# Strided sparse attention into a PReLU feed-forward: batch 0 in another order and layout, weights cast by the DMA, warm-up matmuls

## The chip, the cores and the metric

The kernel runs on one core of a Trainium2 chip. The metric is the device time of one execution in microseconds (us). The kernel before took 391.42 us, the median of three runs from 390.7 to 391.8. A profiled execution of it gives the trace that is read here.

A core has a matrix engine (TensorE, PE in the rows; PEld is its loading of weights), a vector engine (VectorE, DVE), an activation engine (ScalarE, ACT), a general engine (GpSimd, POOL) and an engine that mostly issues transfers (SyncE, SP). Each works through its own instructions in order. Transfers run on 16 DMA engines that all queues share. SBUF is the memory in which all of them work; PSUM is where TensorE writes its results.

## The reference

For 8 batches, 8 heads, 576 positions and a head width of 64, heads 0 to 3 attend locally (a query sees itself and the 31 positions before it) and heads 4 to 7 with a stride (a query sees the positions at or before it that have the same remainder by 32). The result of shape 4608 x 512 goes through a feed-forward with a PReLU.

```python
mask_local = (rel >= 0) & (rel < stride)                       # stride = 32
mask_strided = (rel >= 0) & (pos[None, :] % stride == pos[:, None] % stride)
scores = np.where(masks[None], scale * q @ k.T, -1e9)
attn = softmax(scores) @ v                                     # 8 x 8 x 576 x 64
x = attn.transpose(0, 2, 1, 3).reshape(4608, 512)
h = x @ w_in                                                   # 512 -> 2048
g = np.maximum(h, 0.0) + alpha * np.minimum(h, 0.0)
out = g @ w_out                                                # 2048 -> 512, float32
```

All inputs are float32; the kernel computes its products on float16 operands.

## The kernel before

**Pairs and pieces.** Two heads of a batch make a pair: pairs `4b` and `4b+1` are batch b's local ones, `4b+2` and `4b+3` its strided ones. A pair goes through pieces, and each piece is a handful of instructions on several engines:

- T (`transpose_piece`, L191): TensorE transposes the float16 q or k; ACT copies k into `kT` (L198), DVE copies q into two halves of `qpad` (L202).
- Sc (`score_piece`, L204): scores in PSUM (`sp`, L212), ACT takes the exponential into `et` (L220), and POOL multiplies with a mask (L222, L226). Each pair has three.
- Pv (`pv_piece`, L229): matmuls with v and a column of ones (L240); DVE takes the reciprocal of the sums (L247) and scales (L249). A local pair has two, a strided pair three.
- X (`x_piece`, L254): TensorE transposes the result, and a copy puts it into `xT`, the transposed input of the feed-forward: ACT for a strided pair, with a step of 8 elements in the write (L261), DVE for a local one (L265).

Strided heads are loaded with 8 neighbouring positions in a partition, so that positions that share a remainder by 8 end up in one block of 72; local heads are loaded with position `96 j + p` in partition p, block j.

**Loads.** `load_part` (L102) brings q, k or v of four heads of a batch into a staging tile. Of strided heads it reads runs of 2 KB (8 positions of 64 floats) in two DMAs; of local q and k it reads runs of 256 bytes in four DMAs, one for each head; of local v runs of 256 bytes in five DMAs, with overlapping windows of 128 positions. `cast_part` (L143) casts a staging tile to float16, in two halves. Weights are loaded in four chunks of 1 MB each (`load_w`, L431) into the same ring of seven staging tiles, and cast by DVE, ACT or POOL (`cast_w`, L440).

**Feed-forward.** The 4608 tokens are cut into 9 chunks of 512. `lin1_piece` (L386) computes 128 of the 2048 hidden units for a chunk: four matmuls into one of two `hps` buffers, then ACT writes the negative part (`neg`, L406) and DVE combines both into `gT` (L409), which frees the buffer. `lin2_piece` (L415) computes a quarter of one 128-row tile of the output into `ops`, which has one buffer; after the fourth quarter ACT copies it to SBUF (`osb`, L426) and SP stores it.

**Order.** The order of every engine is that of the program. Ahead of everything come memsets and the loads of batch 0: local q and k on SP, local v on ACT's queue, then strided q, k and v and w_in on SP (L449 to L466). Batch 0's pieces run local pairs first (L287 to L311); POOL's masks and the casts of w_in lie in between. Batch 1's loads are issued on SP after piece 20 and at the end of batch 0, w_out's after them (L494), and batch 2's local ones behind these.

From batch 1 on a fixed rotation (L325 to L366) interleaves the pieces of neighbouring pairs, with POOL's casts for the next data between them; after the second half of a cast the next batch's load of that tile is issued on SP. The first lin1 (chunk 0) is interleaved with batch 1 (L507 to L513), the second with batch 2 (L515 to L519); then lin2 of chunk 0, and from L526 on lin2 of chunk n and lin1 of chunk n+1 alternate with attention. Chunk 1 needs the end of batch 0 and most of batch 1, so lin1 of chunk 1 needs batch 1's last X piece, that of pair 7. By the rotation that piece comes after the scores of pair 8 and the first scores of pair 9.

Of the kernel before, what the change touches and what calls it, by code (L numbers as in the profile page):

```python
# [9 lines left out]
F32 = mybir.dt.float32  # L10
# [20 lines left out]
def kernel(  # L31
# [17 lines left out]
    RING = 4 * S  # L49

# [39 lines left out]
    for i in range(3):  # L90
        keep(nc.vector.memset(qpads[i][64:128, 0, :], 0.0))
        keep(nc.vector.memset(qpads[i][0:64, 1, :], 0.0))
        keep(nc.vector.memset(kTs[i][:, 576:640], 0.0))
    for t in vls + vss:
        keep(nc.gpsimd.memset(t[:, :, :, 64:65], 1.0))
    for t in ets:
        keep(nc.gpsimd.memset(t[:, 384:512], 0.0))
# [4 lines left out]
    def load_part(b, strided, nm, eng=None):  # L102
# [3 lines left out]
        if strided:  # L106
            for lo, hi in ((0, 64), (64, 72)):
                keep(eng.dma_start(
                    st[lo:hi, :].rearrange("p (h e) -> p h e", h=4),
                    src[b, 4:8, 8 * lo : 8 * hi, :].rearrange("h (p t) d -> p h (t d)", t=8),  # L110
                ))
        elif nm != "v":
            for h in range(4):
                keep(eng.dma_start(  # L114
                    st[0:96, 384 * h : 384 * h + 384].rearrange("p (j d) -> p j d", j=6),
                    src[b, h, :, :].rearrange("(j p) d -> p j d", p=96),
                ))
# [25 lines left out]
    def cast_part(b, strided, nm, pr, eng):  # L143

        st = loaded[(b, strided, nm)]
        n = 8 if strided else 6
        np_ = 72 if strided else 96
# [12 lines left out]
        else:  # L160
            if (b, strided, nm) not in cast16:
# [3 lines left out]
            w = 128 * n  # L165
            cast_copy(
                eng,
                t16[0:np_, pr, 0:w].rearrange("p (t h d) -> p t h d", t=n, h=2),
                st[0:np_, w * pr : w * pr + w].rearrange("p (h t d) -> p t h d", h=2, t=n),
# [21 lines left out]
    def transpose_piece(P, which):  # L191
        src = cast16[(P.b, P.strided, which)]
        tp = pspool.tile([128, 1024], F16, tag="ps", name=f"t{which}")
        for t in range(P.n):
            keep(nc.tensor.transpose(  # L195
                tp[:, P.w * t : P.w * t + P.w], src[0 : P.w, P.pr, 128 * t : 128 * t + 128], ident[0 : P.w, 0 : P.w]))
        if which == "k":
            keep(nc.scalar.copy(P.kT[:, 0:576], tp[:, 0:576]))  # L198
        else:
            for hh in range(2):  # L200
                r0 = 64 * hh
                keep(nc.vector.tensor_copy(P.qpad[r0 : r0 + 64, hh, :], tp[r0 : r0 + 64, 0:576]))  # L202

    def score_piece(P, i):  # L204
# [15 lines left out]
        keep(nc.scalar.activation(et[0:r, 0:n], sp[0:r, 0:n], AF.Exp, scale=SCALE))  # L220
        if not P.strided and i == 0:
            keep(nc.gpsimd.tensor_tensor(et[:, 0:n], et[:, 0:n], mfirst, op=ALU.mult))  # L222
        else:
            m = mstr if P.strided else mother
            ev = et[0:r, 0:n].rearrange("r (c f) -> r c f", f=w)
            keep(nc.gpsimd.tensor_tensor(  # L226
# [27 lines left out]
    def x_piece(P):  # L254
# [5 lines left out]
        if P.strided:  # L260
            keep(nc.scalar.copy(  # L261
                xT[:, P.hp, base : base + S].rearrange("r (p t) -> r t p", t=8),
                xp[:, 0:576].rearrange("r (t p) -> r t p", t=8)))
# [23 lines left out]
    for g in (0, 1):  # L287
        feed(T(g, "q"), 0)
        feed(T(g, "k"), 0)
    for i in range(3):  # L290
        feed(Sc(0, i), 0)
    for i in range(3):
        feed(Sc(1, i), 0)
    for g in (0, 1):
        for i in range(2):
            feed(Pv(g, i), 0)
# [3 lines left out]
    feed(X(0), 0)  # L300
    feed(X(1), 0)
# [3 lines left out]
    for g in (2, 3):  # L305
        for i in range(3):
            feed(Pv(g, i), 0)
        if g == 3:
            feed(X(2), 0)
    feed(X(3), 3)  # L310
# [104 lines left out]
    def lin2_piece(n, i):  # L415
        mt, part = i // 4, i % 4
        if part == 0:
            ops_cur["t"] = popool.tile([128, 512], F32, tag="ops", name="ops")
        ops = ops_cur["t"]
        for kf in range(4 * part, 4 * part + 4):  # L420
# [3 lines left out]
        if part == 3:  # L424
            osb = opool.tile([128, 512], F32, tag="osb", name="osb")
            keep(nc.scalar.copy(osb, ops))  # L426
            r0 = 512 * n + 128 * mt
            keep(nc.sync.dma_start(out[r0 : r0 + 128, :], osb))


    def load_w(c, second):  # L431
        st = spool.tile([128, 2048], F32, tag="st", name="wst")
        if second:
            src = moe_w_out[512 * c : 512 * c + 512, :].rearrange("(kf p) c -> p kf c", p=128)
        else:
            src = moe_w_in[:, 512 * c : 512 * c + 512].rearrange("(kk p) c -> p kk c", p=128)
        keep(nc.sync.dma_start(st.rearrange("p (kk c) -> p kk c", kk=4), src))
        return st

    def cast_w(c, second, st, half, eng):  # L440
        s = st.rearrange("p (kk c) -> p kk c", kk=4)[:, 2 * half : 2 * half + 2, :]
        if second:
            o = wout16[:, 4 * c + 2 * half : 4 * c + 2 * half + 2, :]
        else:
            o = win16[:, 2 * half : 2 * half + 2, 512 * c : 512 * c + 512]
        cast_copy(eng, o, s)


    keep(nc.scalar.dma_start(ident, id_dram))  # L449
    load_part(0, False, "q")  # L450
    load_part(0, False, "k")
# [3 lines left out]
    load_part(0, False, "v", nc.scalar)  # L455
    load_part(0, True, "q")
    load_part(0, True, "k")
    load_part(0, True, "v")
    wi = [load_w(0, False)]
    cast_part(0, False, "q", 0, "dve")  # L460
    cast_part(0, False, "k", 0, "act")
    cast_part(0, False, "q", 1, "dve")
    cast_part(0, False, "k", 1, "act")
    cast_part(0, False, "v", 0, "pool")
    cast_part(0, False, "v", 1, "pool")
    wi += [load_w(1, False), load_w(2, False), load_w(3, False)]  # L466
    apt = pspool.tile([128, 512], F32, tag="ps", name="apt")
    keep(nc.tensor.transpose(apt[:, 0:16], alpha_r, id16))
    keep(nc.vector.tensor_scalar(oma, apt[:, 0:16], -1.0, 1.0, op0=ALU.mult, op1=ALU.add))

    for i in range(end0):
        if i == 14:
            cast_part(0, True, "q", 0, "dve")
            cast_part(0, True, "k", 0, "act")
            cast_part(0, True, "q", 1, "dve")
            cast_part(0, True, "k", 1, "act")
            cast_part(0, True, "v", 0, "pool")
            cast_part(0, True, "v", 1, "pool")
        attn_step(end0)
        if i == 20:  # L480
            for nm in ("q", "k", "v"):
                load_part(1, False, nm)
        if i == 24:
            cast_w(0, False, wi[0], 0, "dve")
            cast_w(0, False, wi[0], 1, "act")
    cast_w(1, False, wi[1], 0, "dve")
    cast_w(1, False, wi[1], 1, "act")
    for nm in ("q", "k", "v"):
        load_part(1, True, nm)
    cast_w(2, False, wi[2], 0, "dve")  # L490
    cast_w(2, False, wi[2], 1, "act")
    cast_w(3, False, wi[3], 0, "pool")
    cast_w(3, False, wi[3], 1, "pool")
    wo = [load_w(c, True) for c in range(4)]  # L494
# [4 lines left out]

    for nm in ("q", "k", "v"):  # L500
        for pr in range(2):
            cast_part(1, False, nm, pr, "pool")
        load_part(2, False, nm)
# [3 lines left out]
    for m in range(16):  # L507
        lin1_piece(0, m)
        attn_n(1, end1)
        if m >= 4:  # L510
            attn_n(1, end1)
# [3 lines left out]
    for m in range(16):  # L515
        if m % 2 == 0:
            cast_w(m // 4, True, wo[m // 4], (m // 2) % 2, "pool")
# [48 lines left out]
```

## Time and profile before

| what | before |
|---|---|
| median of 3 runs | 391.42 us (390.7 to 391.8) |
| the profiled execution | 391.96 us |
| its span, first to last instruction | 390.2 us |
| TensorE busy | 329.5 us (84%) |
| ACT, DVE, POOL busy | 213.8, 197.9, 175.8 us |
| moved by DMA | 48.31 MB, mean 124 GB/s |

The profile is of one execution. A row of a group names the line, the engine, the operation and the tiles written and read, then shapes and the count; after the bar come its busy time, the mean of one in ns, and how long the engine idled just before, with what ended the wait. The slices cut the span in 40 equal parts and give tenths of busy time. The chain of waits follows the work that ended last back to the start, each step with its start and length in us. A timeline row gives start and length, and in brackets the idle time before it.

### The profile page before, as it was taken

Reading aid. Unit: us, or ns where it says so; the run is one execution under the profiler, and the core shown is the slowest. Engines: PE = TensorE matmul, PEld = TensorE weight load, DVE = VectorE, ACT = ScalarE, POOL = GpSimd, SP = SyncE. Lnnn points to the kernel's source line nnn. Section 1 sums busy time; section 2 is a strip of 40 time slices with the busy share of each in tenths; the row PEclk is TensorE's granted clock in tenths of the full one; section 3 lists DMA queues with packets and bytes.
Section 4 is the critical chain, followed back from the end, with each engine's and each line's share of the span. In section 5 each row is a group of like instructions: output and inputs, shape, how many; then the busy total and the mean of one; then the engine's idle time right before and its main releaser. Section 6 shows DMA issues by size and latency. Waiting matters only on the chain.

```text
span 390.2 us, 6743 instructions
## 1 busy us (share of the span) xinstructions
PE 329.5 (84%) x2561; PEld 184.2 (47%) x2561; DVE 197.9 (51%) x401; ACT 213.8 (55%) x332; POOL 175.8 (45%) x210
## 2 busy tenths in 40 slices
PE   1464815686899899989998999899899899999985
PEld 1352412353445445555555777455455444444432
DVE  4274505383774346556556566666566444444400
ACT  2466513166565655695677557756955844444411
POOL 1654572789687546556555656665333000000000
PEclk9995778595999999999999999999999999999999
DMA  9998999988499655486558436010000001010021
GB/s 179 200 321 220 217 264 306 211 178 160 108 191 219 144 117 138 112 189 126 126 123 177 110 87 157 21 55 29 28 29 29 27 29 54 27 55 28 27 82 54
DMA packets 80384, 48.31 MB, mean 124 GB/s; under 512 B 64592, under 2 KB 64736, under 8 KB 80352
## 3 DMA queue, kind: packets, MB, share of 16 engines
q1 hardware_dynamic: 76848, 46.94, 51.4%
q10 hardware_dynamic: 3504, 0.95, 1.4%
q8 instruction: 20, 0.33, 0.4%
q14 instruction: 12, 0.10, 0.1%
HBM read 38.43 MB, written 9.44 MB: 123 GB/s over the span
## 4 chain that ended last, share of the span: by engine, by line
PE 67%; DMA 14%; ACT 6%; POOL 5%; DVE 3%; issue 2%; SPq 2%; ACTq 0%; POOLq 0%
PE ops L421 29%; PE hps L396 28%; DMA wst<-in_moe_w_in_dram 5%; DMA stv<-in_v_dram 4%; ACT xT L261 4%; DMA stq<-in_q_dram 3%; PE pv L240 3%; PE sp L212 3%; SPq L114 2%; PE xp L257 2%; DVE gT L409 2%; PE tq L195 2%; DMA stk<-in_k_dram 2%; POOL et L226 2%; PE tk L195 1%
## 5 line engine op out<-in xcount | busy, mean ns | idle before, releaser
L396 PE MATMUL hps<-xT,win 128*128 128x512 f16 (+1 forms) x640 | 156.8, 371 | 11.5 <-ACT xT L261 9.2
L421 PE MATMUL ops<-wout,gT 128*128 128x512 f16 x576 | 145.3, 379 | 4.6 <-ACT osb L426 4.6
L409 DVE SCALAR_TENSOR_TENSOR gT<-neg,oma,hps 128x512 f16<-128x512 f32 x144 | 106.9, 743 | 82.2 <-ACT neg L406 81.5
L406 ACT ACTIVATE neg<-hps 128x512 f32<-128x512 f32 x144 | 88.0, 611 | 92.5 <-PE hps L396 91.6
L226 POOL TENSOR_TENSOR et<-et,masks 128x384 f16<-128x384 f16 (+2 forms) x80 | 72.2, 910 | 77.6 <-ACT et L220 76.9
L396 PEld LDWEIGHTS <-win 128*128 128x128 f16 x640 | 59.6, 101 | 48.1 <-issue 10.3
L421 PEld LDWEIGHTS <-gT 128*128 128x128 f16 x576 | 51.9, 97 | 52.8 <-issue 6.1
L220 ACT ACTIVATE et<-sp 128x384 f16<-128x384 f32 (+2 forms) x96 | 47.7, 510 | 15.3 <-PE sp L212 14.5
L247 DVE RECIPROCAL rc<-pv 96x6 f32<-96x6 f32 (+2 forms) x80 | 15.0, 187 | 71.9 <-PE pv L240 71.8
L261 ACT COPY xT<-xp 128x576 f16<-128x576 f16 x16 | 43.6, 2754 | 13.8 <-PE xp L257 13.3
L240 PEld LDWEIGHTS <-et 72*128 72x128 f16 (+1 forms) x448 | 25.5, 102 | 44.1 <-POOL et L226 18.9
L249 DVE TENSOR_TENSOR x<-pv,rc 96x384 f16<-96x384 f32 (+2 forms) x80 | 42.1, 527 | 2.7
L202 DVE COPY qpad<-tq 64x576 f16<-64x576 f16 x64 | 29.0, 453 | 12.4 <-PE tq L195 11.9
L426 ACT COPY osb<-ops 128x512 f32<-128x512 f32 x36 | 21.0, 585 | 25.6 <-PE ops L421 24.4
L212 PE MATMUL sp<-qpad,kT 128*128 128x144 f16 (+1 forms) x224 | 32.6, 253 | 2.3 <-ACT xT L261 1.9
L212 PEld LDWEIGHTS <-kT 128*128 128x128 f16 x224 | 21.2, 105 | 22.7 <-issue 5.7
L240 PE MATMUL pv<-vl,et 128*128 128x65 f16 x192 | 13.6, 208 | 20.0 <-POOL et L226 14.3
L139 POOL CAST q<-stq 96x768 f16<-96x768 f32 (+1 forms) x28 | 25.4, 929 | 10.9 <-DMA stq<-in_q_dram 8.6
L198 ACT COPY kT<-tk 128x576 f16<-128x576 f16 x32 | 20.4, 637 | 12.4 <-PE tk L195 12.4
L139 POOL CAST k<-stk 96x768 f16<-96x768 f32 (+1 forms) x28 | 26.0, 928 | 1.3 <-DMA stk<-in_k_dram 1.2
L139 POOL CAST vl<-stv 128x768 f16<-128x768 f32 x16 | 13.1, 836 | 14.8 <-DMA stv<-in_v_dram 14.8
L222 POOL TENSOR_TENSOR et<-et,masks 128x384 f16<-128x384 f16 x16 | 14.5, 909 | 11.2 <-ACT et L220 11.2
(29 smaller groups left out, 152.2 us busy)
## 6 DMA issues: line engine op xcount, KB each, us to landing
out_dram<-osb SPq DMA_DIRECT2D x36, 256.0 KB
stq<-in_q_dram SPq DMA_DIRECT2D x32, 144.0 KB
stk<-in_k_dram SPq DMA_DIRECT2D x32, 144.0 KB
stv<-in_v_dram SPq DMA_DIRECT2D x28, 160.0 KB
stq<-in_q_dram SPq DMA_DIRECT2D x8, 512.0 KB
stk<-in_k_dram SPq DMA_DIRECT2D x8, 512.0 KB
stv<-in_v_dram SPq DMA_DIRECT2D x8, 512.0 KB
wst<-in_moe_w_in_dram SPq DMA_DIRECT2D x4, 1024.0 KB
```

Source lines behind the costliest of these rows:

```text
L139: keep(nc.gpsimd.tensor_copy(o, i))
L202: keep(nc.vector.tensor_copy(P.qpad[r0 : r0 + 64, hh, :], tp[r0 : r0 + 64, 0:576]))
L212: keep(nc.tensor.matmul(sp[:, 2 * w * x : 2 * w * x + 2 * w], P.kT[:, k0 : k0 + 128], P.qpad[:, :, w * t : w * t + w], start=(x == 0), sto ...
L220: keep(nc.scalar.activation(et[0:r, 0:n], sp[0:r, 0:n], AF.Exp, scale=SCALE))
L226: keep(nc.gpsimd.tensor_tensor(ev, ev, m.unsqueeze(1).to_broadcast([r, n // w, w]), op=ALU.mult))
L240: keep(nc.tensor.matmul(pv[:, 65 * x : 65 * x + 65], et[0:r, c : c + 128], v16[0:r, t, 2 * P.pr + hh, :], start=(x == 0), stop=(x == nb - ...
L249: keep(nc.vector.tensor_tensor(P.x16[0:w, c0 : c0 + 64 * nb].rearrange("r (c e) -> r c e", e=64), pvv[:, :, 0:64], rc[0:w, 0:nb].unsqueeze ...
L261: keep(nc.scalar.copy(xT[:, P.hp, base : base + S].rearrange("r (p t) -> r t p", t=8), xp[:, 0:576].rearrange("r (t p) -> r t p", t=8)))
L396: keep(nc.tensor.matmul(hps[:, dst : dst + w], win16[:, kk, 128 * m : 128 * m + 128], xT[:, kk, src : src + w], start=(kk == 0 and x == 0) ...
L406: keep(nc.scalar.activation(neg, hps, AF.Relu, scale=-1.0))
L409: keep(nc.vector.scalar_tensor_tensor(gTs[n][:, m, :], neg, oma[:, m : m + 1], hps, op0=ALU.mult, op1=ALU.add))
L421: keep(nc.tensor.matmul(ops, gTs[n][:, kf, 128 * mt : 128 * mt + 128], wout16[:, kf, :], start=(kf == 0), stop=(kf == 15)))
```

## The change

- **Order of batch 0.** The strided pairs (2 and 3) come first, in loads, casts and pieces; the local ones (0 and 1) follow. All six loads go to SP's queue.
- **Layout.** Local q and k are loaded as the strided ones are, in runs of 2 KB and two DMAs. The order of positions is put right when kT and qpad are copied out of PSUM, by reading with a step. The xT copy of strided pairs now reads PSUM with the step and writes in order.
- **Weights.** With `WSW = True`, `load_w` is one DMA on POOL's queue that reads float32 and writes float16 into the final tile; no engine casts weights. The four DMAs of w_in stand between the casts of v of batch 0, those of w_out between POOL's casts of batch 1's local data.
- **Gate.** A small DMA on SP reads 16 columns of w_in's second chunk; batch 1's loads stand behind it on SP.
- **Masks of batch 0** are multiplied on DVE in place of POOL. POOL's memset of `et` is wider (224 columns in place of 128).
- **Warm-up matmuls.** 12 matmuls of 128x512 on a zero tile ahead of the first cast, 4 more after each of the first four pieces, and one after each of the next twelve.
- **lin1 of chunk 0** runs its first 12 pieces with no attention between them; the casts of batch 1's local data and the loads behind them are issued after piece 10. One attention piece follows each of the last four, and the rest of batch 1 comes after that, alone.
- **The last chunk.** lin2's tiles alternate between `ops` and `hps` buffers; the last tile is computed as two halves of 256 columns, each copied by ACT and DVE (128 columns each) and stored by its own DMA.

```diff
-        if strided:
+        if strided or nm != "v":
+            h0 = 4 if strided else 0
             for lo, hi in ((0, 64), (64, 72)):
                 keep(eng.dma_start(
                     st[lo:hi, :].rearrange("p (h e) -> p h e", h=4),
...
+                    src[b, h0 : h0 + 4, 8 * lo : 8 * hi, :].rearrange(
+                        "h (p t) d -> p h (t d)", t=8),
...
+        def move(copy, o, i):
+            if P.strided:
+                keep(copy(o, i))
+            else:
+                keep(copy(o.rearrange("r (p t) -> r p t", t=8),
+                          i.rearrange("r (t p) -> r p t", t=8)))
...
+        eng = nc.vector if P.b == 0 else nc.gpsimd
...
-                xT[:, P.hp, base : base + S].rearrange("r (p t) -> r t p", t=8),
-                xp[:, 0:576].rearrange("r (t p) -> r t p", t=8)))
+                xT[:, P.hp, base : base + S].rearrange("r (p t) -> r p t", t=8),
+                xp[:, 0:576].rearrange("r (t p) -> r p t", t=8)))
...
+            if last and mt % 2 == 1:
+                ops_cur["t"] = phpool.tile([128, 512], F32, tag="hps", name="ops2")
...
+            half = phpool.tile([128, 512], F32, tag="hps", name="ops3") if part else ops
...
+            keep(nc.scalar.copy(osb[:, 0:128], half[:, 0:128]))
+            keep(nc.vector.tensor_copy(osb[:, 128:256], half[:, 128:256]))
+            keep(nc.sync.dma_start(out[r0 : r0 + 128, c0 : c0 + 256], osb[:, 0:256]))
...
     def load_w(c, second):
+        if WSW:
+            keep(nc.gpsimd.dma_start(w_dst(c, second), w_src(c, second)))
+            return
...
+    def warm(n):
+        for _ in range(n):
+            keep(nc.tensor.matmul(wps, wrm[:, 0:128], wrm, start=True, stop=True))
...
+    for nm in ("q", "k", "v"):
+        load_part(0, True, nm)
+    for nm in ("q", "k", "v"):
+        load_part(0, False, nm)
...
+    def cast_qk(b, strided):
+        cast_part(b, strided, "q", 0, "dve")
+        cast_part(b, strided, "k", 0, "act")
+        cast_part(b, strided, "q", 1, "dve")
+        cast_part(b, strided, "k", 1, "dve")
+
+    warm(12)
+    cast_qk(0, True)
+    cast_part(0, True, "v", 0, "pool")
+    cast_part(0, True, "v", 1, "pool")
+    if WSW:
+        load_w(0, False)
     cast_part(0, False, "v", 0, "pool")
+    if WSW:
+        load_w(1, False)
     cast_part(0, False, "v", 1, "pool")
+    if WSW:
+        load_w(2, False)
+        load_w(3, False)
...
+        if i == 16:
+            cast_qk(0, False)
         attn_step(end0)
+        if i < 4:
+            warm(4)
+        elif i < 16:
+            warm(1)
...
+    if WSW:
+        gate = cpool.tile([128, 16], F16)
+        keep(nc.sync.dma_start(gate, win16[:, 0, 1008:1024]))
+    for strided in (False, True):
+        for nm in ("q", "k", "v"):
+            load_part(1, strided, nm)
...
     for m in range(16):
...
         lin1_piece(0, m)
+        if m == 10:
+            for nm in ("q", "k", "v"):
+                for pr in range(2):
+                    cast_part(1, False, nm, pr, "pool")
+                load_part(2, False, nm)
+                if WSW:
+                    load_w("qkv".index(nm), True)
+            if WSW:
+                load_w(3, True)
+        attn_n(0 if m < 12 else 1, end1)
```

More of the change, by code (lines that the diff above doesn't have):

```diff
@@ L284, in X @@
         return lambda: x_piece(pairs[g])
[L287 to L296, printed above, removed]
     for g in (2, 3):
@@ L496, in attn_n @@
+    for strided in (False, True):
+        for nm in ("q", "k", "v"):
+            load_part(1, strided, nm)
+    if not WSW:
+        for c in range(4):
+            load_w(c, True)
     def attn_n(n, end):
```

168 lines of the change are left out of this document (81 added, 87 removed).

## The prediction

> **What bounds the kernel now.** I read the slices of the page first, then cut the span into stages, and then asked the chain of waits what each stage hangs on. The slices:
>
> ```profile
> span 390.2 us, 6743 instructions
> PE   1464815686899899989998999899899899999985
> POOL 1654572789687546556555656665333000000000
> DMA  9998999988499655486558436010000001010021
> ```
>
> TensorE (PE) is full from slice 13 to the end and half idle before; DMA is full in the first ten slices (98 us). The stages, by busy time (columns: stretch, length, then PE, PEld, DVE, ACT, POOL, granted clock, DMA share, GB/s):
>
> ```profile
> 0.00:10.00 10.00, 1.91 (x19) 1.56 (x19) 3.93 (x14) 2.12 (x2) 1.89 (x16) 1.00 0.97 180
> 20.00:30.00 10.00, 6.36 (x82) 5.57 (x80) 7.71 (x18) 6.58 (x11) 5.98 (x7) 1.00 1.05 331
> 38.20:95.50 57.30, 33.98 (x278) 19.42 (x278) 25.80 (x54) 25.72 (x42) 39.10 (x46) 0.74 1.04 226
> 95.50:117.00 21.50, 19.56 (x143) 10.32 (x143) 15.21 (x28) 12.37 (x24) 16.22 (x18) 0.93 0.80 145
> 117.00:137.50 20.50, 18.00 (x155) 9.88 (x153) 7.46 (x19) 11.96 (x15) 12.88 (x15) 1.00 0.84 185
> 137.50:308.00 170.50, 164.56 (x1467) 97.71 (x1467) 104.31 (x218) 113.79 (x178) 90.57 (x101) 1.00 0.39 94
> ```
>
> DMA is busy in both of the first two rows, but with 256-byte runs (0 to 10) it moves 180 GB/s, and with mostly 2 KB runs (20 to 30) 331. From 38.2 to 95.5, TensorE works 34 of 57 us; from 137.5 on it is full. So time is to be won ahead of about 137. The chain, cut to the steps that carry it:
>
> ```profile
> 1.18 3.81 DMA stq<-in_q_dram
> ...
> 17.27 20.02 DMA wst<-in_moe_w_in_dram
> ...
> 40.85 1.72 PE hps L396 x4
> 44.95 10.96 DMA stv<-in_v_dram
> ...
> 63.16 6.86 DMA stq<-in_q_dram
> ...
> 88.54 1.99 POOL vs L139 x2
> ...
> 92.74 2.73 ACT xT L261
> ...
> 138.70 0.86 PE hps L396 x4
> ```
>
> Loads carry it to about 70 us: w_in until 37.3, batch 1's strided v until 55.9, batch 2's q (queued behind w_out) until 70.0. Then POOL carries it (casts and masks). At 92.74 + 2.73 = 95.5 the first half of the sequence ends: batch 1's last xT is written, and the second chunk of lin1 can be finished. The same four matmuls take 1.72 us at 40.85 and 0.86 at 138.70; the first is the slow clock.
>
> **The change part by part.** The costs of one instruction:
>
> ```profile
> L409 DVE SCALAR_TENSOR_TENSOR gT<-neg,oma,hps 128x512 f16<-128x512 f32 x144 | 106.9, 743 | 82.2 <-ACT neg L406 81.5
> L406 ACT ACTIVATE neg<-hps 128x512 f32<-128x512 f32 x144 | 88.0, 611 | 92.5 <-PE hps L396 91.6
> L261 ACT COPY xT<-xp 128x576 f16<-128x576 f16 x16 | 43.6, 2754 | 13.8 <-PE xp L257 13.3
> L226 POOL TENSOR_TENSOR et<-et,masks 72x432 f16<-72x432 f16 x32 | 32.0, 1003 | 13.1 <-ACT et L220 12.4
> L202 DVE COPY qpad<-tq 64x576 f16<-64x576 f16 x64 | 29.0, 453 | 12.4 <-PE tq L195 11.9
> L226 POOL TENSOR_TENSOR et<-et,masks 128x384 f16<-128x384 f16 x32 | 29.0, 909 | 38.8 <-ACT et L220 38.8
> L198 ACT COPY kT<-tk 128x576 f16<-128x576 f16 x32 | 20.4, 637 | 12.4 <-PE tk L195 12.4
> L249 DVE TENSOR_TENSOR x<-pv,rc 72x384 f16<-72x384 f32 x32 | 17.7, 553 | 1.1
> L139 POOL CAST vs<-stv 72x1024 f16<-72x1024 f32 x16 | 16.4, 1048 | 4.1 <-DMA stv<-in_v_dram 4.1
> L139 POOL CAST k<-stk 72x1024 f16<-72x1024 f32 x14 | 14.5, 1035 | 1.2 <-DMA stk<-in_k_dram 1.2
> L139 POOL CAST vl<-stv 128x768 f16<-128x768 f32 x16 | 13.1, 836 | 14.8 <-DMA stv<-in_v_dram 14.8
> L139 POOL CAST wout<-wst 128x1024 f16<-128x1024 f32 x8 | 8.3, 1036 | 0.0
> L247 DVE RECIPROCAL rc<-pv 72x6 f32<-72x6 f32 x32 | 6.0, 189 | 14.7 <-PE pv L240 14.7
> L137 DVE CAST q<-stq 72x1024 f16<-72x1024 f32 x2 | 1.3, 680 | 0.0
> ```
>
> *Loads.* A load is 0.59 MB, or 1.8 us at 331 GB/s; local v keeps 256-byte runs (0.79 MB, 4.4 us at 180). The first load of before took 3.81 us for half of that, so strided q is there at about 5.1, k at 6.9, v at 8.7, local q and k at 10.5 and 12.2, v at 17 to 19 beside the first weights. w_in (4.2 MB, 12.7 us at 331) is issued by POOL behind the strided and local v casts: chunk 0 at about 11, the others at 20 to 23; chunk 1 lands at about 25, the last at about 32. The new wait, SP's little DMA that reads win16, holds all fifteen of batch 1's DMAs until chunk 1 is there. Nobody needs them sooner: by bytes (two v at 180, 12.2 MB at 331, with half of w_out in between) they are complete at about 49, and batch 2's, which share with the rest of w_out, at about 69.
>
> *Eight DMAs on POOL's queue.* No row shows a DMA that POOL issues, nor a cast in flight. The nearest for the issue is SP's pair below: 0.68 us each; I bound it by 0.5 and 2.2 (the row of four, its waits included) and take 1, so 8 us. Against it POOL loses ten weight casts of 1.04 us. For the transfer I take the rate of the 2 KB loads (it reads the same runs and writes half), with half that rate as the other end.
>
> ```profile
> 9.98 1.36 SPq L108 DMA_DIRECT2D stk<-in_k_dram  x2
> 12.97 8.85 SPq L437 DMA_DIRECT2D wst<-in_moe_w_in_dram  x4
> ```
>
> *Batch 0.* The memsets that move behind the loads, the wider one of et on POOL and the transpose of alpha lie beside the wait for the first load or for k; without that cover they cost 2 us together. The casts of w_in leave DVE, ACT and POOL, where they stood at the end of this stage. The 12 warm-up matmuls (0.43 us each by the 1.72 row) end at about 6.3, when strided q has just been cast. The other 28 cost 0.22 to 0.43 each; four behind each transpose piece push the first score from about 9 to 12, which k's casts and copies cover in part. Scores end at 15, DVE's six masks at 16. No row has a mask on DVE; two-input work there takes 553 ns for 384 elements (L249), copies of 16-bit data 453 for 576, so 0.3 to 0.62; I take 0.45. Six times L247 + L249 (0.74) end at 20.3. Local pairs: three casts to 22.3, four qpad moves, masks, four times 0.74 and two X copies on DVE: 32.
>
> *Strided reads.* Local kT and qpad, and strided xT, now read PSUM with a step and write in order. L261, the only element-wise stepped copy, takes 2754 ns where the same size in order takes 637 (L198); there the write has the step. Which side costs the 2.1 us no row tells. [...] I take 0.64 and 0.7: what L261 shows as slow is a copy with a stepped write, and the new ones have none. [...]
>
> *lin1 of chunk 0* loses its interleaving: 12 pieces stand alone. With two hps buffers a piece costs half of PE 0.86 + ACT 0.61 + DVE 0.74 + about 0.2 of hand-over, so 1.2 us: 32 + 14.4 = 46.4. Batch 1's first score is three pieces later, its mask at 51.
>
> *Batch 1, now without lin1 beside it*, is POOL's: per pair three masks (2.73 us) and three casts (2.5 to 3.1; local q and k casts are 72x1024 now, 1.04 each). Pairs 4 to 7 take 5.9, 5.8, 5.4 and 5.8, and 2.9 of pair 8's lie ahead of batch 1's last transpose: 25.8, so 76.8; four PE pieces and an xT copy of 0.64 make 79.5. DMA is close behind (batch 2's strided v is there at 69 and is wanted at 72). Against 95.5: **-16.0**.
>
> *lin1 of chunk 1, lin2 of chunk 0.* TensorE idles 21.5 - 19.6 + 20.5 - 18.0 = 4.4 us there, with POOL casting w_out. Those casts go; POOL still has the masks. I take **-1.7**, between 0 and -4.4.
>
> *xT stalls and the end*, from the waits (total, times, longest) and the timeline:
>
> ```profile
> PE hps L396 <- ACT xT L261: 9.2, 7, 2.0
> ```
>
> ```profile
> 35.67 0.58 PE L396 MATMUL hps<-xT,win 128*128 128x512 f16 x1 [1.28 <-ACT xT L261]
> 38.23 0.59 PE L396 MATMUL hps<-xT,win 128*128 128x512 f16 x1 [1.97 <-ACT xT L261]
> 95.51 0.58 PE L396 MATMUL hps<-xT,win 128*128 128x512 f16 x1 [1.53 <-ACT xT L261]
> ...
> 374.41 3.61 PE L421 MATMUL ops<-wout,gT 128*128 128x512 f16 x16 [0.67 <-ACT osb L426]
> 386.72 0.58 ACT L426 COPY osb<-ops 128x512 f32<-128x512 f32 x1 [3.75 <-PE ops L421]
> ```
>
> Of the 9.2 us, 1.28 + 1.97 + 1.53 = 4.8 lie in the first two batches; four stalls of 1.1 remain, gone with the short copy: **-4.4**. In the last chunk three waits of 0.67 to 0.72 for osb fall away, since the tiles alternate, and the last copy of 0.58 is split: **-2.4**.
>
> **Sum.** The profiled execution took 391.96 us (span 390.2 and 1.76 around it; the median is 391.42, 0.1% less). 391.96 - 16.0 - 1.7 - 4.4 - 2.4 = 367.5.
>
> **Rivals.** *Stepped PSUM reads cost what L261 costs.* Then the 4.4 stays, X(7) ends 2.1 later, four copies of batch 0 put 8.5 on ACT ahead of the exps (about 6 not covered by DVE), and local kT stalls a little in each batch (2): 382. For it: L261's 3.7 ns an element more; against: its write is stepped too. [...]
>
> *Cast in flight is slow: slower than before.* At half rate the eight MB cost 25 us more of a DMA stage that just fits; batch 2 lands some 15 later and the first term goes: 382. It decides the sign where the last w_in chunk comes later than the first term and the others can pay, at about 71 us: 4.2 MB in 59 us, 71 GB/s. At 50 GB/s it lands at 96 and lin1 stands there: 392 + 25 = 417. For it: not one packet of before went through a software queue; against: 2 KB runs at 331 GB/s leave a factor of four. [...]
>
> *The start is shorter than that.* If DVE's masks cost 0.3 and POOL casts ahead of its masks while lin1 runs, batch 0 ends at 28 and batch 1 needs 20 us: 355. For it: POOL is free from 24 to 31; against: casts wait in one queue with masks.
>
> *The early gain is given back*: TensorE is no sooner full, because batch 1 alone takes as long as with lin1 beside it: 391.
>
> **How the numbers follow.** The sum 0.52 (own range 358 to 377); stepped reads 0.15; shorter start 0.13; half-rate casts 0.06; still slower casts 0.10; given back 0.04. The range 352 to 386 holds the first nearly whole and most of the next three, about 0.8. Within 0.3% (1.2 us, what a measurement of this kernel tells from no change) 0.03, slower 0.10, faster 0.87. The predicted time is 367.
>
> **What would show it.** Strided q cast near 5.5 us; w_in complete near 32; batch 0's last X copy near 32; lin1 pieces of chunk 0 at 1.2 us; POOL full from 51 to 77; xT and local kT copies at 0.64 us; lin1 of chunk 1 starting near 79.5; no osb wait in the last chunk. It is wrong if w_in lands after 46, if the stepped copies take 2.7 us, or if POOL waits for loads between 51 and 77.

## The result and the profile after

The changed kernel takes 376.61 us (median of 4 runs, 375.11 to 378.22), the kernel before 391.13 beside it: ratio 0.963, 95% interval [0.959, 0.967]. That is 14.5 us less; the forecast was 24.4 less, at 367. The profiled execution took 378.22, the highest of the four, 1.6 above the median; its span is 376.5 against 390.2. The page's first line and four of its slices:

```profile
span 376.5 us, 6946 instructions
PE   6768874566899999999999999999999999999996
POOL 2321646899546646557655666865433000000000
DMA  7999999999997645377547736011000001001012
GB/s 154 187 182 175 180 216 223 187 200 171 197 174 172 163 119 133 107 167 178 125 112 160 158 92 154 29 41 46 29 30 30 28 28 57 28 28 57 29 57 84
```

From the twelfth slice on (9.4 us each) TensorE's digit is 9 up to the last slice; before, eights come between. DMA is still nearly full in the first twelve slices, and it moves 154 to 223 GB/s there. The windows, cut at the ends of the changed kernel's stages (columns as in the prediction):

```profile
10.00:24.50 14.50, 10.75 (x97) 6.12 (x97) 8.09 (x24) 5.76 (x10) 4.42 (x5) 0.78 1.18 186
24.50:36.00 11.50, 8.74 (x98) 6.52 (x99) 10.52 (x24) 4.83 (x10) 2.25 (x3) 0.59 1.03 167
36.00:56.50 20.50, 16.83 (x75) 6.67 (x74) 11.89 (x16) 8.89 (x15) 10.53 (x12) 0.90 1.18 202
56.50:92.27 35.77, 19.70 (x225) 15.19 (x224) 16.92 (x38) 12.58 (x25) 30.79 (x34) 0.56 1.12 196
92.27:132.60 40.33, 36.95 (x300) 19.95 (x299) 23.88 (x46) 20.45 (x38) 23.88 (x26) 0.97 0.89 178
132.60:300.00 167.40, 167.35 (x1514) 99.34 (x1514) 110.89 (x219) 98.78 (x180) 93.24 (x101) 1.00 0.39 97
```

The last row is the visible gain: TensorE idles for 0.05 us, where the row of before (137.5 to 308) left 5.94 idle. In the third and fourth rows, lin1 of chunk 0 and batch 1, little was won. The chain of waits says why:

```profile
45.93 15.41 DMA stv<-in_v_dram
...
61.35 12.19 DMA stv<-in_v_dram
...
74.10 7.58 DMA stk<-in_k_dram
...
81.83 1.04 POOL k L132
...
90.53 1.71 PE hps L394 x4
```

Loads carry it until 81.7, twelve us longer than before (70.0): batch 1's strided v, then batch 2's v and k. I mark the start of chunk 1 by ACT's first `neg` of it, since every kernel has that row; before it stands at 96.13. ACT's timeline after, with the last xT copy of batch 1 ahead of it:

```profile
90.56 0.64 ACT L261 COPY xT<-xp 128x576 f16<-128x576 f16 x1 [3.87 <-PE xp L257]
92.27 0.60 ACT L404 ACTIVATE neg<-hps 128x512 f32<-128x512 f32 x1 [1.07 <-PE hps L394]
```

Chunk 1 starts 3.9 us sooner, where 16.0 were forecast. The other 9.8 of the 13.7 us between the two spans come after it: 1.0 up to the start of chunk 1's lin2 (137.52 before, 132.63 after), 6.5 from there to the last chunk, of which 5.9 were idle time of TensorE, and 2.35 in the last chunk. The groups by form show the copies at the price taken, and the new masks below it:

```profile
L261 ACT COPY xT<-xp 128x576 f16<-128x576 f16 x16 | 10.2, 639 | 11.5 <-PE xp L257 11.1
L191 ACT COPY kT<-tk 128x576 f16<-128x576 f16 x16 | 10.2, 638 | 14.9 <-PE tk L185 14.9
L193 DVE COPY qpad<-tq 64x576 f16<-64x576 f16 x32 | 24.1, 753 | 2.1 <-PE tq L185 1.9
L226 DVE TENSOR_TENSOR et<-et,masks 128x384 f16<-128x384 f16 x4 | 1.4, 358 | 0.2
L462 POOL DMA_DIRECT2D win<-in_moe_w_in_dram x4 | 3.2, 790 | 0.0
```

### The profile page after: what moved, and what is told of

The parts are those of the page before. It is cut to its first block, busy times and chain, and to the rows that moved or that the text cites. A ratio compares the mean times of both kernels' runs of the same rounds, so it can differ in the third digit from the quotient of the medians.

```text
span 376.5 us, 6946 instructions
## 1 busy us (share of the span) xinstructions
PE 339.6 (90%) x2681; PEld 190.4 (51%) x2681; DVE 212.4 (56%) x415; ACT 181.1 (48%) x328; POOL 167.6 (45%) x196
## 4 chain that ended last, share of the span: by engine, by line
PE 75%; DMA 11%; DVE 6%; ACT 3%; POOL 2%; issue 1%; SPq 1%; ACTq 0%; POOLq 0%; DVEq 0%
PE ops L439 32%; PE hps L394 30%; DMA stv<-in_v_dram 7%; DMA stk<-in_k_dram 4%; PE sp L211 3%; PE pv L240 3%; PE xp L257 2%; DVE gT L407 2%; DVE x L249 2%; PE tk L185 2%; PE tq L185 2%; PE wps L478 1%; PE ops L430 1%; ACT neg L404 1%; ACT et L219 1%
## 5 line engine op out<-in xcount | busy, mean ns | idle before, releaser
L226 POOL TENSOR_TENSOR et<-et,masks 128x384 f16<-128x384 f16 (+2 forms) x70 | 63.2, 907 | 70.6 <-ACT et L219 69.8
L247 DVE RECIPROCAL rc<-pv 72x6 f32<-72x6 f32 (+2 forms) x80 | 14.9, 186 | 54.0 <-PE pv L240 53.9
L249 DVE TENSOR_TENSOR x<-pv,rc 72x384 f16<-72x384 f32 (+2 forms) x80 | 42.1, 527 | 2.7
L240 PEld LDWEIGHTS <-et 72*128 72x128 f16 (+1 forms) x448 | 26.4, 104 | 29.1 <-POOL et L226 14.5
L132 POOL CAST q<-stq 72x1024 f16<-72x1024 f32 x28 | 28.2, 1036 | 11.6 <-DMA stq<-in_q_dram 11.6
L132 POOL CAST k<-stk 72x1024 f16<-72x1024 f32 x28 | 28.9, 1035 | 5.5 <-PE tk L185 2.8
L193 DVE COPY qpad<-tq 64x576 f16<-64x576 f16 x32 | 24.1, 753 | 2.1 <-PE tq L185 1.9
L132 POOL CAST vs<-stv 72x1024 f16<-72x1024 f32 x16 | 16.4, 1048 | 12.3 <-DMA stv<-in_v_dram 12.3
L240 PE MATMUL pv<-vs,et 72*128 72x65 f16 x256 | 16.9, 200 | 2.6 <-POOL et L226 2.6
L185 PE MATMUL tq<-ident,q 72*128 72x72 f16 x256 | 15.1, 207 | 4.3 <-DVE q L130 4.3
L185 PEld LDWEIGHTS <-q 72*128 72x128 f16 x256 | 13.1, 105 | 10.2 <-DVE q L130 5.4
```

Of the source, the lines that this page charges most:

```text
L132: keep(nc.gpsimd.tensor_copy(o, i))
L185: keep(nc.tensor.transpose(tp[:, 72 * t : 72 * t + 72], src[0:72, P.pr, 128 * t : 128 * t + 128], ident[0:72, 0:72]))
L193: keep(copy(o.rearrange("r (p t) -> r p t", t=8), i.rearrange("r (t p) -> r p t", t=8)))
L226: keep(eng.tensor_tensor(ev, ev, m.unsqueeze(1).to_broadcast([r, n // w, w]), op=ALU.mult))
L240: keep(nc.tensor.matmul(pv[:, 65 * x : 65 * x + 65], et[0:r, c : c + 128], v16[0:r, t, 2 * P.pr + hh, :], start=(x == 0), stop=(x == nb - ...
L249: keep(nc.vector.tensor_tensor(P.x16[0:w, c0 : c0 + 64 * nb].rearrange("r (c e) -> r c e", e=64), pvv[:, :, 0:64], rc[0:w, 0:nb].unsqueeze ...
```

## The experiments

Each diff is against the changed kernel unless it says otherwise. Both loads-only kernels (the first and the fifth) leave out all computation and store zeros.

**Loads alone.** Groups of two to four loads of each form in a row; DVE closes each load with a small copy of one of its columns.

> This kernel computes nothing of the reference and stores zeros: it only loads, in eight groups, each waited for before the next, to measure the rate of each kind of load alone. Theory 'placement' (the rate of a load hangs on which partitions it fills, so that 64 of 128 partitions get about half): (1) four loads as in the changed kernel, partitions 0-63 and 64-71, 2.36 MB: 13.8 us; (2) partitions 0-31 and 32-63, 2.10 MB: 12.3 us; (3) the same rows into partitions 0-31 and 64-95: 6.5 to 7.5 us; (4) 96 partitions with runs of 1.5 KB, 2.36 MB: 9 to 10 us. Rival 'runs' (2 KB runs get 331 GB/s, and the loads were slow in the kernel because of what else moved): (1) 7.1 us, (2) 6.3, (3) 6.3, (4) about 7.5. Both: (5) 96 partitions in 256-byte runs 13 us, (6) the w_in chunks through SP 12.7 us, (7) the same through POOL with the cast 13 to 14 us, (8) two local v, 1.57 MB, 8.7 us.

The first two groups can't be read: POOL's software DMAs waited for nothing, and their four weight transfers ran beside them. In the later groups only loads of SP's queue run. Landings in DVE's timeline: three loads of the third group (the same rows in two DMAs, into partitions 0 to 31 and 64 to 95), then two successive loads of 96 partitions in 256-byte runs, then two of local v:

```profile
33.55 0.14 DVE L56 COPY fl<-st 1x1 f32<-1x1 f32 x1 [0.83 <-DMA st<-in_q_dram]
35.80 0.14 DVE L56 COPY fl<-st 1x1 f32<-1x1 f32 x1 [2.10 <-DMA st<-in_k_dram]
38.08 0.14 DVE L56 COPY fl<-st 1x1 f32<-1x1 f32 x1 [2.14 <-DMA st<-in_q_dram]
...
59.42 0.15 DVE L56 COPY fl<-st 96x1 f32<-96x1 f32 x1 [2.70 <-DMA st<-in_q_dram]
62.23 0.15 DVE L56 COPY fl<-st 96x1 f32<-96x1 f32 x1 [2.66 <-DMA st<-in_k_dram]
...
76.12 0.15 DVE L56 COPY fl<-st 128x1 f32<-128x1 f32 x1 [0.20 <-DMA st<-in_v_dram]
79.69 0.15 DVE L56 COPY fl<-st 128x1 f32<-128x1 f32 x1 [3.42 <-DMA st<-in_v_dram]
```

A local q or k as before loads it takes 2.81 us, 210 GB/s; local v 3.57 us, 220. Short runs were not as slow as the 180 GB/s of the first ten us had made me think. The third group missed its forecast: 0.52 MB land every 2.2 to 2.3 us, so four take about 9, where 'placement' said 6.5 to 7.5. With one DMA into each half of the partitions a load gets no more than some 235 GB/s.

**Local q and k back in 96 partitions**, with 6 positions each (1.5 KB runs, one DMA), all else as changed:

```diff
+        if not strided and nm != "v":
+            keep(eng.dma_start(
+                st[0:96, 0:1536].rearrange("p (h e) -> p h e", h=4),
+                src[b, 0:4, :, :].rearrange("h (p t) d -> p h (t d)", t=6)))
...
```

> The changed kernel with local q and k in 96 partitions of 6 positions (runs of 1.5 KB, one DMA) in place of 72 partitions of 8. Theory 'placement': each of these loads takes 2.6 us in place of 3.45, so batch 0 ends 1.7 us sooner and batch 1's and 2's data by 1.7 each; POOL's local casts shrink from 1.04 to 0.82 us; lin1 of chunk 1 starts 3 to 5 us sooner: 372 to 374. Rival 'runs': the loads take as long as before or a little longer, the shorter casts bring at most 1: 375 to 377.

372.26 us, ratio 0.954 [0.950, 0.957]; chunk 1 at 87.51, 4.8 us sooner. POOL's row in batch 1's stage:

```profile
57.00:87.00 30.00, 17.47 (x193) 13.68 (x191) 15.95 (x37) 11.07 (x23) 29.22 (x34) 0.57 1.09 213
```

POOL works 29.2 of the 30 us: now it is the limit there. Two of a batch's six loads in other partitions (their casts are shorter too, 0.82 us in place of 1.04, and a transpose piece has six matmuls in place of eight) bring 4.4 us more.

**w_out's loads behind lin1 of chunk 1** (after its first four pieces, not beside batch 1's loads; the issues at piece 10 go):

```diff
         lin1_piece(1, m)
+        if m < 4:
+            load_w(m, True)
```

> The changed kernel with the four loads of w_out issued behind the first four pieces of lin1 of chunk 1 in place of between the casts of batch 1. If w_out's 4.2 MB (13 us of transfer) hold up batch 1's strided and batch 2's local loads ('share'), lin1 of chunk 1 starts 7 to 10 us sooner, w_out still lands before lin2 needs it, and the time is 367 to 370. If those loads are limited by their own target partitions and w_out only uses what they leave ('placement'), it is 374 to 377; if w_out then comes too late for lin2, 377 to 385.

376.42 us, 0.966 [0.961, 0.970]. Chunk 1 starts at 87.54, 4.7 sooner, so w_out does compete with batch 1's loads. But the chain now has

```profile
92.34 21.38 DMA wout<-in_moe_w_out_dram
```

and lin2 waits for it until 113.7: all of the gain is given back.

**Weights through staging and casts on the engines**, as before:

```diff
-    WSW = True
+    WSW = False
```

> The changed kernel with the weights loaded by SP as float32 and cast by DVE, ACT and POOL, all else as it is. 'Casting in flight brings much': 16 casts of 0.7 to 1.15 us come back, the first of them ahead of lin1: 380 to 386. 'It brings nothing, the loads of q, k and v set the pace': 374 to 379, since w_out then stands behind batch 1's loads on SP.

383.39 us, 0.982 [0.979, 0.985]; chunk 1 at 97.17. By the medians casting in flight is worth 6.8 us in this kernel, together with the order of loads that comes with it: without it there is no gate, and w_out stands on SP behind batch 1's loads.

**Loads alone, each group behind the end of the one before.** In order: 64 partitions 0 to 63; 64 partitions 32 to 95; 128; the kernel's form (64 + 8); 96; weights by SP; weights with the cast by POOL.

```python
keep(nc.sync.dma_start(st[0:64, :].rearrange("p (r e) -> p r e", r=8), flat(src, 64, 8)))
...
keep(nc.sync.dma_start(st[32:96, :].rearrange("p (r e) -> p r e", r=8), flat(src, 64, 8)))
```

> Loads alone again, stores zeros, computes nothing of the reference; this time each of seven groups starts only when the one before has wholly landed, the cast transfers too. Groups 1 to 3 read the same rows of 2 KB, three times 1.05 MB: into partitions 0-63, into 32-95, into 0-127. Theory 'placement by halves' (partitions 0-63 and 64-127 are served by different halves of what takes the data, and a load that fills one half gets half the rate): 1 takes 14 to 15 us, 2 and 3 take 8 to 9. Rival 'few partitions' (64 partitions are slow wherever they lie): 1 and 2 take 14 to 15, 3 takes 8 to 9. Rival 'the rows of q are slow to read': all three 12 to 15. Group 4 is the form of the changed kernel (0-63 and a second transfer for 64-71, 0.59 MB each): 10.3 us for three if the second transfer adds its quarter to some of the engines (the kernel's 3.45 us each), 8.4 if not. Group 5, 96 partitions in runs of 1.5 KB: 7.3. Group 6, w_in on SP, 3.15 MB: 8.3 to 9. Group 7, the same through POOL with the cast: 8.5 to 10 if the cast costs nothing, 16 or more if it halves the rate.

DVE's timeline, the second and third landing of the first three groups and the last two of the cast:

```profile
14.09 0.14 DVE L56 COPY fl<-st 64x1 f32<-64x1 f32 x1 [4.75 <-DMA st<-in_k_dram]
18.84 0.15 DVE L56 COPY fl<-st 64x1 f32<-64x1 f32 x1 [4.61 <-DMA st<-in_q_dram]
...
29.05 0.14 DVE L56 COPY fl<-st 32x1 f32<-32x1 f32 x1 [2.52 <-DMA st<-in_k_dram]
31.66 0.15 DVE L56 COPY fl<-st 32x1 f32<-32x1 f32 x1 [2.47 <-DMA st<-in_q_dram]
...
40.31 0.15 DVE L56 COPY fl<-st 128x1 f32<-128x1 f32 x1 [2.53 <-DMA st<-in_k_dram]
42.97 0.15 DVE L56 COPY fl<-st 128x1 f32<-128x1 f32 x1 [2.50 <-DMA st<-in_q_dram]
...
83.88 0.15 DVE L56 CAST fl<-w 128x1 f32<-128x1 f16 x1 [2.39 <-DMA w<-in_moe_w_in_dram]
86.44 0.15 DVE L56 CAST fl<-w 128x1 f32<-128x1 f16 x1 [2.40 <-DMA w<-in_moe_w_in_dram]
```

The same 1.05 MB in the same 2 KB runs takes 4.75 us in partitions 0 to 63 (221 GB/s), 2.61 in 32 to 95 (402), and 2.66 in all 128 (394). So it is not the number of partitions but which ones. The kernel's form takes 2.9 us for 0.59 MB (201 GB/s), 96 partitions 2.1 (281; the mean of 2.38 and 1.82), weights by SP 2.69 (390), and with the cast 2.56 (410): the cast costs the transfer nothing. Whether 64 to 127 have a way in of their own is not shown: no run loads them alone.

**w_out between batch 1's pieces**, with local q and k in 96 partitions. The diff is against that kernel, whose four issues at piece 10 go:

```diff
+        if j1 in (10, 14, 18, 22):
+            load_w((j1 - 10) // 4, True)
```

> The changed kernel with local q and k in 96 partitions of 6 positions, and w_out's four loads issued one by one between batch 1's pieces (after 10, 14, 18 and 22 of the forty that stand alone), so later than in the changed kernel and sooner than behind lin1 of chunk 1. 'Share': each of the two moved the first result of chunk 1 from 92.3 to 87.5; together they bring it to 83 to 85, w_out lands before lin2 asks for it, and the time is 366 to 369. If the one limit hides the other (POOL's queue is full by then): 370 to 372. If w_out is late again: 372 to 376.

374.39 us, 0.958 [0.953, 0.964], and chunk 1 at 88.76, 1.25 later than without the move. POOL was already full there, and the four issues of 0.81 us each are its work too. The two ratios' intervals overlap, so the times alone don't tell a loss:

```profile
57.00:88.00 31.00, 17.38 (x195) 13.04 (x193) 16.15 (x37) 11.19 (x23) 30.96 (x36) 0.54 1.10 200
```

**The kernel before with the xT copy's flip alone** (diff against the kernel before):

```diff
-                xT[:, P.hp, base : base + S].rearrange("r (p t) -> r t p", t=8),
-                xp[:, 0:576].rearrange("r (t p) -> r t p", t=8)))
+                xT[:, P.hp, base : base + S].rearrange("r (p t) -> r p t", t=8),
+                xp[:, 0:576].rearrange("r (t p) -> r p t", t=8)))
```

> The kernel before with one part of the change: the xT copy of strided pairs reads PSUM with a step and writes in order. By the prediction's term the copy takes 0.64 us in place of 2.75, the four stalls of 1.1 us in the full stage go, and some of the 4.8 us in the first two batches: -4.4 to -7, so 384 to 387. If the stalls are only replaced by the next wait: 389 to 391.

379.80 us, 0.971 [0.967, 0.975]: 11.1 us from two lines. Chunk 1 starts at 91.42, 4.7 sooner, and this window stands against that of before with 164.56:

```profile
137.50:308.00 170.50, 170.48 (x1476) 100.04 (x1475) 107.90 (x221) 99.60 (x181) 88.54 (x99) 1.00 0.37 91
```

**No warm-up matmuls:**

```diff
-        for _ in range(n):
+        for _ in range(0):
```

> The changed kernel without its 40 warm-up matmuls. If the loads set the pace to 82 us, as the chain of waits says, nothing changes: 375.5 to 377.5, though batch 0 may end up to 3 us sooner. If batch 0's own chain counts, the four matmuls behind each transpose piece cost it 3 us: 373 to 374.5. If they pay by a faster clock: 378 to 381.

375.49 us, 0.961 [0.957, 0.965], which can't be told from the changed kernel (0.963 [0.959, 0.967]). The windows differ, though. Without the matmuls:

```profile
10.00:24.50 14.50, 8.43 (x106) 7.17 (x107) 12.21 (x28) 6.28 (x11) 4.78 (x5) 1.00 1.16 200
24.50:36.00 11.50, 9.72 (x75) 6.01 (x73) 8.52 (x21) 4.78 (x10) 2.26 (x3) 1.00 1.08 186
```

The granted clock is 1.00 in both, where the changed kernel has 0.78 and 0.59. But lin1's first matmuls are as slow with the one as with the other: the first two `neg` are 1.71 us apart in both kernels, and the chain without the warm-ups has

```profile
33.44 4.74 PE hps L394 x11
```

which is 0.43 us for each matmul, as slow as before in the row of 1.72 for four, at a granted clock that reads 1.00. So the warm-ups do not make lin1's start faster, and the clock's figure can't be taken at its word in this stretch. Ahead of lin1 they do quicken some matmuls: the 32 transposes of batch 0's q take 214 ns in the mean with them and 254 without. But in these two executions they cost more than that. Without them lin1's first `neg` comes at 34.92 in place of 37.37, and chunk 1 starts at 89.18 in place of 92.27; of these 3.1 us the medians keep 1.1.

**q and k loads moved by 32 partitions**, to 32 to 103; the casts read 40 of the 72 rows, so that 32 are left out of the result. The new fp16 buffers and their zeroing are left out of the diff here:

```diff
-                    st[lo:hi, :].rearrange("p (h e) -> p h e", h=4),
+                    st[P0 + lo : P0 + hi, :].rearrange("p (h e) -> p h e", h=4),
...
-                t16[0:72, pr, :].rearrange("p (t h d) -> p t h d", t=8, h=2),
-                st[0:72, 1024 * pr : 1024 * pr + 1024].rearrange(...),
+                t16[0:40, pr, :].rearrange("p (t h d) -> p t h d", t=8, h=2),
+                st[64:104, 1024 * pr : 1024 * pr + 1024].rearrange(...),
```

> [...] Bytes, runs, issues and order of the loads stay. Theory (the halves of the partitions limit the loads: 218 GB/s at 0 to 63, 399 at 32 to 95 in the loads-only kernel): the strided q and k of batch 0 take some 2 us each in place of 3.45, the strided k cast comes near 8.5 to 9 in place of 10.7, the first neg of chunk 1 near 85 to 89 in place of 92.3, and the time is 369 to 373. Rival (the short chunks of the eight-row rest, or the issuing, set the pace): nothing moves, chunk 1 stays at 91 to 93 and the time at 375 to 378.

371.60 us, 0.954 [0.950, 0.958]; POOL's first mask at 54.52 in place of 59.54, chunk 1 at 85.54 in place of 92.27. Bytes, runs and order of the loads are those of the changed kernel. Besides the partitions one thing differs: DVE zeroes the buffers first, so that the warm-up matmuls start at 5.48 in place of 1.19, and two of the four groups that follow the first transposes take half their time. The second group in the changed kernel, then here:

```profile
12.30 1.90 PE L478 MATMUL wps<-wrm 128*128 128x512 f16 x4
...
11.34 1.03 PE L484 MATMUL wps<-wrm 128*128 128x512 f16 x4
```

Batch 0 ends 2.9 us sooner (32.9 in place of 35.85). Of these 1.5 are the loads' (ACT casts the strided k at 9.19 in place of 10.73), and 1.4 go with the matmuls; so up to 1.4 of the 6.7 us at chunk 1 need not come from the partitions. In the chain from 33 to 85 us no load appears any more, and batch 1's stage is POOL's:

```profile
54.00:85.54 31.54, 18.17 (x220) 14.32 (x219) 17.01 (x38) 11.96 (x25) 30.14 (x33) 0.60 1.10 212
```

**The kernel before with the flip and the last chunk's pieces alone:** the diff of the seventh, and `lin2_piece` as changed.

> The kernel before with two parts of the change alone: the xT copy's flip and the last chunk's output pieces. Theory (the start is worth nothing as it was built; the two terms add up): 379.8 for the flip alone less 2.35 that the tail showed, 377.2 to 377.7; the rest of the change, all that it does to the start, is then worth 1 us or less. Rival (the tail is hidden, or the start brought part of the 14.5): 379 to 380.

376.83 us, 0.968 [0.964, 0.972] beside 0.963 [0.959, 0.967] for the whole change; chunk 1 at 92.27, to the hundredth where the changed kernel has it (whose profiled execution was 1.6 above its median, this one at its median). The rest of the change, its whole new start, is worth some 0.5% by the two ratios, and with their intervals it can't be told from nothing.

**The changed kernel with the old stepped write of xT:** the diff of the seventh backwards.

> The changed kernel with the xT copy's old stepped write, all else as changed. Theory (the flip is worth 11.1 us wherever it stands): xT copies of 2.75 us again, PE idle of some 6 us between 160 and 320, chunk 1 some 4 us later at 96 to 97, time 386 to 388.5. Rival (in the changed kernel the start is set by loads, so that the copies there are hidden and only the later stages pay): chunk 1 stays at 92 to 93 and the time is 382 to 385. Second rival (the flip was one of several that each remove the same stall): 377 to 379.

387.16 us, 0.993 [0.990, 0.995], so the flip is worth 10.6 us here as well. The time is the theory's, but not the place: chunk 1 comes at 93.86, nearer to the first rival's 92 to 93 than to 96 to 97, so that in the changed start most of the copy's length is hidden behind loads. By the spans 1.6 of 9.8 us are lost before chunk 1 and 8.2 after it, where TensorE waits again:

```profile
137.50:300.00 162.50, 158.03 (x1442) 94.15 (x1441) 105.05 (x208) 108.85 (x173) 92.98 (x101) 1.00 0.41 96
```

**Attention begun sooner**, on the kernel with 96 partitions and without warm-ups:

```diff
-        if m == 10:
+        if m == 2:
...
-        attn_n(0 if m < 12 else 1, end1)
+        attn_n(0 if m < 6 else 1, end1)
```

> The changed kernel with local q and k in 96 partitions, no warm-up matmuls, and batch 1's attention begun at piece 6 of lin1 chunk 0 in place of piece 12, its POOL casts at piece 2 in place of 10. Theory (in the 96-partition kernel POOL works without a gap from its first mask at 57.9 to 87, and stands idle for 10 of the 20 us before it, so that its stage can begin as soon as local v has been cast, near 50): first mask at 50 to 52, chunk 1 at 80 to 83, time 365 to 368. Rival (loads set the pace: strided q, k and v of batch 1 land as before, near 53, 56 and 60): chunk 1 at 85 to 88, time 370 to 373.

371.26 us, 0.952 [0.948, 0.955]. It beats both kernels and is the fastest that was run, but not by a difference that can be told from the 96-partition kernel alone (0.954 [0.950, 0.957]). Here the rival held: chunk 1 at 85.18, since POOL's timeline waits for loads again and its first mask comes at 54.85:

```profile
49.43 2.02 POOL L136 CAST q<-stq 72x1024 f16<-72x1024 f32 x2 [2.67 <-DMA stq<-in_q_dram]
...
54.85 0.90 POOL L228 TENSOR_TENSOR et<-et,masks 128x384 f16<-128x384 f16 x1
...
57.77 1.05 POOL L136 CAST vs<-stv 72x1024 f16<-72x1024 f32 x1 [1.04 <-DMA stv<-in_v_dram]
```

## Why the prediction was right or wrong

The sign was right, and 376.6 lies in the range, at the very edge of the likeliest case's own (358 to 377): 9.1 us of the gain that the sum gave are missing. That it lies there is in part luck: the largest term brought a quarter of its size, and the smaller ones, the xT copy's above all, brought more than was put down for them. Term by term, by the spans of the two profiled executions (that of the changed kernel lay 1.6 above its median):

| term | forecast | measured |
|---|---|---|
| start of chunk 1 | -16.0 | -3.9 |
| lin1 of chunk 1, lin2 of chunk 0 | -1.7 | -1.0 |
| xT stalls after it | -4.4 | -6.5 |
| last chunk | -2.4 | -2.35 |

**The step that failed is the price of a load**: "0.59 MB, or 1.8 us at 331 GB/s". The 331 is a window of before in which w_in moved, into 128 partitions, and I put it down to the 2 KB runs. The strided q and k loads are 3.5 us apart in the changed kernel (DVE's casts begin at 7.28 and 10.74) and 2.9 alone; what adds the rest in the kernel no run shows. The part "2 KB runs for all of q and k" thus brought two things that cancel by the rates of the loads-only kernels: longer runs, and a move of local q and k from 96 partitions (210 GB/s even in 256-byte runs) to 64 + 8 (201).

From there the delay can be followed through the steps. Batch 0's last X copy ends at 35.85, not 32. lin1's first twelve pieces are through at 52.9, not 46.4: between 44 and 53, where the granted clock is 1.00, a piece takes 1.245 us (1.2 forecast), and slow first ones add some 2. The first mask comes at 59.54, not 51, and from it to POOL's last mask ahead of the last transpose it takes 29.7, not 25.8, with loads in between. "POOL full from 51 to 77" and "complete at about 49" for batch 1 both fail on the load: its strided v lands at 61.3. POOL waits for q, v and k there (1.23 us before 53.62, 1.18 before 62.61, 1.56 before 71.65), which the prediction had named as a sign that it is wrong. The run with q and k moved by 32 partitions bears this out: with no load left in the chain, the stages come within 1, 3.5 and 6 us of the forecast (32.9, 54.5, 82.5), and chunk 1 starts 6.7 us sooner, up to 1.4 of which may be the warm-ups'. What is left of the 16.0, 5.4 us, is the smaller slips of the engines' own steps, the first lin1 pieces and the POOL stage (28.0, of which POOL worked 27.2; forecast 25.8).

**The xT stalls** were the right mechanism, and the waits that name the copy have the size taken (4.5 us after 137.5). The sum left out that the copy also holds up what stands behind it on ACT. Two more waits of the kernel before come from that:

```profile
124.68 2.74 ACT L261 COPY xT<-xp 128x576 f16<-128x576 f16 x1 [2.29 <-PE xp L257]
128.26 1.02 PE L421 MATMUL ops<-wout,gT 128*128 128x512 f16 x4 [1.27 <-ACT osb L426]
...
303.35 2.73 ACT L261 COPY xT<-xp 128x576 f16<-128x576 f16 x1 [0.72 <-PE xp L257]
307.89 0.24 PE L257 MATMUL xp<-ident,x 72*128 72x72 f16 x2 [1.47 <-DVE x L249]
```

At 128.26 TensorE waits for an osb copy that stood behind the xT copy. At 307.89 it waits for DVE, which had itself waited for a `neg` behind the xT copy. With the flip alone the first wait is 0.23 us and the second is gone.

So the second row of the table is near its forecast by luck. Its 1.7 were to come from w_out's casts, which leave POOL. But the flip alone, with these casts still in place, shortens this stretch by 1.8 us (91.42 to 131.00, where it was 96.13 to 137.52).

Alone the flip is worth 11.1, since it also brings chunk 1 forward by 4.7. In the prediction that part was to come out of the rearranged start, and so the term hid that the flip is most of the change.

**The other steps.** Stepped PSUM reads were free on ACT (638 and 639 ns, 637 in order before), and cost DVE 0.30 (753 against 453 in order before): the first rival falls. The 0.7 us that batch 0's sum took for each of DVE's four qpad copies was my estimate, and no run of before shows it; the changed kernel's row has 0.753 in its place. Casting in flight had the rate taken (410 GB/s against 331), so the second rival falls with both of its ends; POOL's issue was 0.74 to 0.79, less than the 1 taken. DVE's masks cost 0.36 (0.45 taken), so the third rival's first condition (0.3) was nearly met, but the start was not shorter, since loads set it. The fourth, "the early gain is given back", had 4% and comes nearest to what the new start did, but for another reason than the one given: slow loads, not batch 1 alone on the engines. Without the cast in flight the new start would have lost some 6 us (ratio 0.982 against 0.968 for the flip and the last chunk alone). In the last chunk no wait for osb is left; from the first row below to the end are 17.74 us, where the same stretch took 20.1 before (370.1 to 390.2):

```profile
358.76 10.52 PE L439 MATMUL ops<-wout,gT 128*128 128x512 f16 x48
369.12 3.66 PE L430 MATMUL ops<-wout,gT 128*128 128x256 f16 x32
```

**Still open:** the clock. It reads 0.54 to 0.60 in batch 1's stage in each window of it shown here, 1.00 where matmuls take twice their time, and the runs do not say what sets either.

## What to carry to other kernels

Take a load's rate from a row with the same partitions, not only the same runs or bytes: a window's GB/s is a mix of all that moved (here 331, and 201 for the load alone). In a change of many parts put one part alone into the kernel before; here two lines gave 11 of the 14.5 us, the last chunk 2.4, and the new start nearly nothing. When a limit is lifted, look at once for the next (loads, then POOL, then w_out): a move that pays under the one can bring nothing under the other.

## What was not expected of the hardware

- 1.05 MB in 2 KB runs: 221 GB/s into partitions 0 to 63, 402 into 32 to 95, 394 into 128.
- Run length mattered less than that: 210 GB/s for 256-byte runs in 96 partitions (four DMAs), 281 for 1.5 KB runs in the same 96 (one DMA), and 201 for 2 KB runs in 64 + 8.
- Two DMAs, into 0 to 31 and 64 to 95, moved some 235 GB/s, far below one DMA into 32 to 95.
- A software DMA that casts float32 to float16 reads at 410 GB/s, against 390 for the same weights without a cast.
- A copy of 576 float16 values on ACT takes 2754 ns when it writes SBUF with a step of 8 elements, and 639 when it reads PSUM with a step of 72 and writes in order.
- Forty warm-up matmuls on zeros went with a granted clock of 0.78 and 0.59 between 10 and 36 us, and their absence with 1.00; lin1's first matmuls took 0.43 us each at that 1.00, and at 138.70 in the kernel before four take 0.86 (0.215 each) at the same 1.00.
